# Where four DMA transpositions of the second attention step stand in SP's queue

## The chip, the cores and the metric

The kernel runs on one core of one Trainium2 chip. The metric is the device time of one execution in microseconds, as the median of several runs. The engines are TensorE (PE), VectorE (DVE), ScalarE (ACT), GpSimd (POOL) and SyncE (SP); here SP does nothing but issue DMAs, and POOL nothing but issue loads after its first few microseconds.

## What is computed

Eight sequences of 3072 rows go through an attention without softmax, gated by u, and then through a two-branch maxout layer:

```python
scores = (1/S) * z @ z.T            # S = 3072, z has 64 columns
attn   = maximum(scores, 0) ** 2
x      = u * (attn @ v)             # u and v have 256 columns
h      = maximum(x @ w1, x @ w2)    # 1024 columns
out    = h @ w_out                  # 256 columns
```

The inputs and the output are float32; the products are made in bfloat16 with float32 sums.

## The kernel before, in words

**Tiles.** A sequence is cut into 24 blocks of 128 rows, and these into 6 groups of 4 blocks. A step is one group of output rows of one sequence; there are 48, counted from n = 0, and steps 0 to 5 belong to the first sequence. Step n needs attn between its own 4 blocks and all 24 blocks of the sequence, group by group.

**Symmetry.** The scores are symmetric. Only the part on and above the diagonal is made on PE (`add_pair`, `add_diag`); ACT and DVE apply the maximum and the square, which leaves a tile `a_sb` for each step and group. A later step that needs the mirrored tile gets it by a DMA transposition, issued by SP (`do_turn`, through `sp_dma`, L83), into a tile `aT`. One transposition turns two blocks, so step n makes T(n,k) and T(n,k+2) for a group g with k = 4g, and step g reads them. For the first sequence, steps 0 to 2 make their tiles among each other directly and are added up plainly (`add_plain`). From step 3 on, the products run through a scheme with seven products in place of eight: DVE makes sums of the tiles (`add_sums`, the jobs S1 to S4 in `es`) and differences of v (`add_fold`, in `lf`), and PE makes products X (three a piece, from the tiles) and Y (four a piece, from the tiles and the sums).

**The other transpositions on SP.** Each step's u is turned (`uT`); the second weight is turned once (`w2T`), because PE multiplies it with w_out at the start (`w2o`); each later sequence's z is turned into `zT`, from which its scores are made; the diagonal group of each step is turned in place in two small pieces. SP also issues the stores of the output, 512 KB each. The loads (v, u, z and the weights) are issued by POOL (L87) and most of them wait for a given matmul (`timed`).

**Order.** The order of PE's work is written out by hand (`work`, `laid`, giving `pe_order`). All other jobs are put in order by a planner at the end of the function: each job has a cost, a lag and a due time worked out backwards from PE's plan, and the planner hands each engine the job that is ready first and, among those, the one due first. SP takes its jobs strictly in that order.

**Buffers.** A job that takes a new tile of a pool waits until all jobs of the tile that had the buffer are done, and takers of a pool follow each other in the order written in `order`. The pool of `aT` has 12 buffers (`NT`). Its order comes from a sorted list, `slots`: each turned group has a place in PE's order as its key, and so have the second weight (`w2`, `w2T`) and the two tiles of step 0's groups 4 and 5, which are kept in this pool (`a_held`) until they are turned late. Because the takers follow each other, a place in `slots` is also a place in SP's order.

The function `held` picks step 0's groups 4 and 5; their key is the place of PE 1 us into step 2, in the plan's time. All other groups have the place of the first score that makes them.

Of the kernel before, what the change touches and what calls it, by code (L numbers as in the profile page):

```python
# [11 lines left out]
def kernel(  # L12
# [29 lines left out]
    G = 4  # L42
# [215 lines left out]
    def a_key(n, g):  # L258
        return ("T", ("held", n, g)) if n < HELD and g > 3 else ("A", (n, g))
# [734 lines left out]
    for i, w in enumerate(work):  # L994
        key = w[2]
# [44 lines left out]
    def pe_job_at(ns):  # L1040
        found = [key for key, at in zip(pe_order, pe_at) if at >= ns]
        return [found[0]] if found else [pe_order[-1]]


    def at_step(b, s, us):
        return pe_job_at(starts[NG * b + s] + us * 1000)
# [160 lines left out]
    for pool in ("acc0", "acc1"):  # L1207
        order[pool].sort(key=lambda k: k[0] * 2 + k[1] if isinstance(k, tuple) else 2 * k)
    position = {key: i for i, key in enumerate(pe_order)}
    order["A"].sort(  # L1210
        key=lambda k: position.get(("score", k[0], None if k[1] == steps[k[0]].s and steps[k[0]].diag else G * k[1]), -1)
    )
    def held(key):
        return a_key(key[1], key[2] // G)[0] == "T"

    slots = sorted(
        [
            (position[at_step(0, key[1] + 2, 1)[0]] if held(key) else position.get(key, -1), k)
            for key, k in turned_order
        ]  # L1220
        + [(position.get(key, -1), ("held", key[1], k[2])) for key, k in turned_order if held(key)]
# [1 line left out]
        key=lambda x: x[0],  # L1223
# [210 lines left out]
```

## Time and profile before

| | |
|---|---|
| time, median of 3 runs | 932.8 us (932.5 to 934.61) |
| the profiled execution | 930.27 us |
| its span, first to last instruction | 928.5 us |
| PE busy | 923.0 us (99%) |
| DVE busy | 766.3 us (83%) |
| ACT busy | 682.2 us (73%) |
| POOL busy | 58.4 us (6%) |
| granted TensorE clock | 1.000 |
| mean DMA flow | 154 GB/s |
| transpositions `aT` issued by SP | 230, median 4.2 us to landing |
| transpositions `uT` | 48, median 4.6 us to landing |
| loads of v, of u | 48 each, 256 KB, median 5.3 us to landing |

The profile is one execution. Busy is the time in which an engine executes instructions; matmuls overlap each other, and their ends are modelled, so PE's waits are better read from the distances between starts. "Landing" is the moment at which a DMA's completion is told. SP's rows in the timeline give the time that SP spends on issuing a DMA; the data lands later. A window row gives, for a stretch of time, the busy time of each engine with its number of instructions, then the granted clock, the mean busy share of the 16 DMA engines and the flow in GB/s.

### The profile page before, as it was taken

How to read it: one execution, taken by the hardware profiler on the slowest of the kernel's cores; microseconds unless marked ns; L12 is line 12 of the kernel's file. 1: busy time of each engine (PE TensorE's matmuls, PEld its weight loads, DVE VectorE, ACT ScalarE, POOL GpSimd, SP SyncE). 2: the span in 40 equal slices, each digit the busy share in tenths (PEclk: the TensorE clock that was granted, in tenths of full speed). 3: DMA queues.
4: the chain of work that ended last, by engine and by line, in shares of the span. 5: the costliest groups of instructions: out<-in, count | busy, mean ns of one | idle time of the engine just before them, and what ended most of it. 6: DMA issues, size and time to landing. Idle time of an engine off the chain costs nothing.

```text
span 928.5 us, 18994 instructions
## 1 busy us (share of the span) xinstructions
PE 923.0 (99%) x7343; PEld 668.2 (72%) x7343; DVE 766.3 (83%) x1915; ACT 682.2 (73%) x825; POOL 58.4 (6%) x115
## 2 busy tenths in 40 slices
PE   9999999999999999999999999999999999999998
PEld 3367777777777777777777776777767776777786
DVE  7958997888978888888888888888898887988761
ACT  8867876778777777776877678776888658875634
POOL 2100100000000000001000010000000000000000
PEclk9999999999999999999999999999999999999999
DMA  9999999987989879998999899988898888986611
GB/s 161 151 183 180 179 186 181 158 156 136 160 172 157 151 137 180 165 152 144 151 188 153 153 146 158 172 150 153 144 166 173 149 149 149 183 154 125 121 46 68
DMA packets 372778, 142.54 MB, mean 154 GB/s; under 512 B 351184, under 2 KB 352848, under 8 KB 372688
## 3 DMA queue, kind: packets, MB, share of 16 engines
q1 hardware_dynamic: 356128, 111.60, 64.6%
q0 software_dynamic: 16560, 29.74, 22.9%
q8 instruction: 57, 0.93, 0.4%
q14 instruction: 33, 0.27, 0.1%
HBM read 59.77 MB, written 25.17 MB: 91 GB/s over the span
## 4 chain that ended last, share of the span: by engine, by line
PE 94%; DVE 3%; DMA 1%; issue 0%; ACT 0%; POOL 0%; POOLq 0%
PE s_ps L80 47%; PE acc L80 47%; DVE es L233 1%; DMA v_sb<-in_v_dram 1%; DVE a_sb L221 1%; DVE lf L236 0%; DMA o_sb<-in_z_dram 0%; DVE a_sb L233 0%; DVE xT L240 0%; DVE e L233 0%; DVE a_sb L227 0%; DVE g_sb L221 0%; DVE e L236 0%; ACT a_sb L225 0%; ACT a_sb L219 0%
## 5 line engine op out<-in xcount | busy, mean ns | idle before, releaser
L80 PEld LDWEIGHTS <-v_sb 128*128 128x128 bf16 x2304 | 223.7, 98 | 79.9 <-issue 37.7
L219 ACT ACTIVATE a_sb<-s_ps 128x1024 bf16<-128x1024 f32 (+1 forms) x231 | 211.6, 971 | 30.7 <-PE s_ps L80 28.0
L225 ACT ACTIVATE a_sb<-a_sb 128x1024 bf16<-128x1024 bf16 (+1 forms) x220 | 214.2, 1010 | 0.3
L80 PE MATMUL acc<-es,v_sb 128*128 128x256 bf16 x864 | 197.4, 274 | 0.1
L80 PE MATMUL s_ps<-w_out_sb,g_sb 128*128 128x256 bf16 x1504 | 195.0, 273 | 0.0
L219 ACT ACTIVATE g_sb<-s_ps 128x1024 bf16<-128x1024 f32 x181 | 170.9, 1029 | 13.4 <-PE s_ps L80 13.4
L233 DVE TENSOR_TENSOR es<-a_sb 128x512 bf16<-128x512 bf16 x306 | 121.1, 416 | 66.9 <-PE acc L80 66.9
L80 PEld LDWEIGHTS <-lf 128*128 128x128 bf16 x1620 | 158.3, 98 | 22.6 <-issue 0.3
L80 PE MATMUL s_ps<-xT,w_sb 128*128 128x512 bf16 x768 | 173.6, 379 | 0.0
L80 PE MATMUL acc<-es,lf 128*128 128x256 bf16 x756 | 170.8, 273 | 0.0
L80 PE MATMUL acc<-a_sb,lf 128*128 128x256 bf16 x612 | 166.9, 273 | 0.0
L80 PEld LDWEIGHTS <-g_sb 128*128 128x128 bf16 x1504 | 146.9, 98 | 17.5
L80 PE MATMUL acc<-aT,v_sb 128*128 128x256 bf16 x684 | 143.0, 273 | 0.0
L80 PE MATMUL acc<-a_sb,v_sb 128*128 128x256 bf16 (+1 forms) x740 | 138.9, 291 | 0.3 <-ACT a_sb L225 0.3
L80 PEld LDWEIGHTS <-w_sb 128*128 128x128 bf16 x768 | 75.0, 98 | 81.1 <-issue 0.3
L230 ACT COPY e<-acc 128x512 f32<-128x512 f32 x90 | 53.2, 591 | 108.9 <-PE acc L80 108.5
L221 DVE TENSOR_SCALAR a_sb<-s_ps 128x1024 bf16<-128x1024 f32 (+1 forms) x107 | 121.2, 1133 | 5.1 <-PE s_ps L80 4.8
L230 ACT COPY o_sb<-s_ps 128x512 f32<-128x512 f32 (+1 forms) x92 | 53.1, 577 | 86.3 <-PE s_ps L80 86.3
L80 PE MATMUL s_ps<-zT 64*128 64x512 bf16 (+1 forms) x684 | 92.9, 366 | 0.4 <-DVE zT L110 0.4
L227 DVE TENSOR_TENSOR a_sb<-a_sb 128x1024 bf16<-128x1024 bf16 (+1 forms) x118 | 75.0, 647 | 0.2 <-ACT a_sb L219 0.2
L80 PE MATMUL s_ps<-W2o_sb,xT 128*128 128x256 bf16 x384 | 73.4, 273 | 0.0
L80 PE MATMUL acc<-aT,lf 128*128 128x256 bf16 x252 | 68.7, 273 | 0.0
(60 smaller groups left out, 711.8 us busy)
## 6 DMA issues: line engine op xcount, KB each, us to landing
out_dram<-o_sb SPq DMA_DIRECT2D x47, 512.0 KB, 3.7
v_sb<-in_v_dram POOLq DMA_DIRECT2D x48, 256.0 KB, 5.3
u_sb<-in_u_dram POOLq DMA_DIRECT2D x48, 256.0 KB, 5.3
aT<-a_sb SPq DMA_TRANSPOSE x230, 4.2
z_sb<-in_z_dram POOLq DMA_DIRECT2D x7, 384.0 KB, 5.4
a_sb<-a_sb SPq DMA_TRANSPOSE x90, 3.2
w_sb<-in_moe_w_dram POOLq DMA_DIRECT2D x2, 512.0 KB, 9.6
uT<-u_sb SPq DMA_TRANSPOSE x48, 4.6
```

The source lines that it names most:

```text
L80: newest[0] = pin(nc.tensor.matmul(*args, **kw)).ins
L219: pin(nc.scalar.activation(out_ap, in_ap, AF.Relu))
L221: pin(nc.vector.tensor_single_scalar(out=out_ap, in_=in_ap, scalar=0.0, op=ALU.max))
L225: pin(nc.scalar.activation(ap, ap, AF.Square))
L227: pin(nc.vector.tensor_mul(ap, ap, ap))
L230: pin(nc.scalar.copy(out_ap, in_ap) if eng == "ACT" else nc.vector.tensor_copy(out_ap, in_ap))
L233: pin(nc.vector.tensor_add(*args))
```

## The change

Step 1's groups 4 and 5, which had the place of their first score as key, now get the place of PE 1.5 us into step 2. Step 0's groups 4 and 5 get the place 4 us into step 2 in place of 1 us. Everything else of the source stays.

```diff
     def held(key):
         return a_key(key[1], key[2] // G)[0] == "T"
 
+    LATE = (4, 1.5)
+
+    def late(key):
+        return key[1] < 2 and key[2] // G > 3
+
     slots = sorted(
         [
-            (position[at_step(0, key[1] + 2, 1)[0]] if held(key) else position.get(key, -1), k)
+            (position[at_step(0, 2, LATE[key[1]])[0]] if late(key) else position.get(key, -1), k)
             for key, k in turned_order
         ]
         + [(position.get(key, -1), ("held", key[1], k[2])) for key, k in turned_order if held(key)]
```

What SP issues early, in the order of both kernels ("d3" is step 3's pair of small diagonal transpositions, "w2" the second weight, "u2" the u of step 2, "s0" the store of step 0's output, "zT" two DMAs):

```
before: T(1,12) T(1,16) T(1,14) T(1,20) w2 u2 T(1,18) T(2,12) T(2,14) T(1,22) T(2,16) T(0,16) d3
        T(0,18) T(2,18) T(0,20) u3 T(0,22) u4 s0 T(2,20) T(3,16) T(3,18) d4 zT T(2,22) T(3,20)
        T(3,22) T(4,20) d5 s1 u5 T(4,22) d6 T(6,4) T(6,8) s2 u6 T(6,12) T(6,16) T(6,20)
after:  T(1,12) T(1,14) w2 u2 T(2,12) T(2,14) T(2,16) T(1,16) T(1,18) d3 T(1,20) T(1,22) T(2,20)
        T(0,16) T(0,18) T(2,18) u3 T(2,22) s0 u4 T(0,20) T(3,16) T(3,18) d4 zT T(0,22) d5 s1 u5
        T(3,20) T(3,22) T(4,20) T(4,22) d6 T(6,4) s2 T(6,8) T(6,12) u6 T(6,16) T(6,20)
```

The 12 buffers of the `aT` pool go round in the new order too: the tile of (step 0, group 5) now takes the buffer of (step 0, group 3), which step 3 reads first, in place of (step 2, group 5), and (sequence 1, step 0, group 3) no longer takes a buffer that step 5 reads.

## The prediction

> A transposition is written T(n,k) below: SP's DMA that turns blocks k and k+1 of step n; steps, groups and blocks count from 0, so the second step is n = 1.
>
> **What bounds the kernel now.** I read the page first: busy shares, then the chain that ended last.
>
> ```profile
> PE 923.0 (99%) x7343; PEld 668.2 (72%) x7343; DVE 766.3 (83%) x1915; ACT 682.2 (73%) x825; POOL 58.4 (6%) x115
> ...
> PE 94%; DVE 3%; DMA 1%; issue 0%; ACT 0%; POOL 0%; POOLq 0%
> ```
>
> TensorE is busy for 99% of the span and is 94% of the chain. A busy PE can still be waiting, because matmul ends are modelled, so the list of waits and then the start-to-start distances of the matmuls come next.
>
> ```profile
> PE zeros L80 <- DVE blank L144: 1.2, 1, 1.2
> PE s_ps L80 <- DVE zT L110: 0.4, 1, 0.4
> PE tpz L109 <- DVE z_sb L154: 0.3, 1, 0.3
> PE acc L80 <- ACT a_sb L225: 0.3, 1, 0.3
> ```
>
> All of PE's listed waits lie in the first 10 us. In the timeline of PE after that, two 256-column matmuls take 0.38 us. I looked for pairs that take longer, in the whole span:
>
> ```profile
> 130.40 0.38 PE L80 MATMUL acc<-es,v_sb 128*128 128x256 bf16 x2
> 130.62 0.27 PE L80 MATMUL acc<-a_sb,lf 128*128 128x256 bf16 x1
> 130.73 0.27 PE L80 MATMUL acc<-es,lf 128*128 128x256 bf16 x1
> 130.84 0.63 PE L80 MATMUL acc<-es,v_sb 128*128 128x256 bf16 x2
> ```
>
> The last pair lost 0.25 us. Besides it there are 0.18 us at 123.7 and 0.08 us at 68.2, and nothing else above the constant price of switching between scores and products. So stalls that could go are worth 0.51 us in this execution, and anything beyond that must come from losses which it does not show.
>
> **The time to sum against.** The profiled execution took 930.27 us (span 928.50 and 1.77 around it). The median of the runs is 932.8, 2.5 above it, and they spread over 2.1 (932.5 to 934.61). I take differences from the profile and add them to the median.
>
> **The change, part by part.** The order views of both kernels show PE, ACT and POOL unchanged; DVE has the same instructions with five of them moved by one place or a few; SP has the same DMAs in another order up to T(6,16). So no work is added or removed: everything is about when SP's transpositions land. These are SP's issues now (start, duration):
>
> ```profile
> 25.35 7.53 SPq L83 DMA_TRANSPOSE aT<-a_sb  x4
> 32.98 8.72 SPq L83 DMA_TRANSPOSE w2T_sb<-w_sb  x1
> 41.78 1.26 SPq L83 DMA_TRANSPOSE uT<-u_sb  x1
> 43.14 10.66 SPq L83 DMA_TRANSPOSE aT<-a_sb  x5
> ...
> 63.09 2.57 SPq L83 DMA_TRANSPOSE uT<-u_sb  x1
> ...
> 76.72 4.81 SPq L83 DMA_TRANSPOSE zT<-z_sb  x2
> 81.58 8.14 SPq L83 DMA_TRANSPOSE aT<-a_sb  x4
> ```
>
> *Step 1, the head of the queue.* Today T(1,12), T(1,16), T(1,14), T(1,20) go ahead of the second weight. With T(1,16) and T(1,20) gone from there, the weight's transposition moves from 33.0 to about 28.1 (its load landed at 26.7), and the third u's follows it (load landed at 31.6). Then SP meets T(2,12), whose square ends on DVE at 39.0: four finished transpositions of step 1 now stand behind that wait. Their users are far: DVE first reads T(1,16) and T(1,18) at 73.3, for step 4, and T(1,20) and T(1,22) at 92.5, for step 5; the four will land by about 58 (nine issues from 39.1 on, priced as below). Cost 0, hidden by at least 15 us.
>
> *Step 2, up to the next sequence's zT.* zT is the transposition with the least margin: its second half lands at 86.38 and PE's score row starts at 86.66, 0.28 us later. In the new order SP has 22 instructions from T(2,12) up to zT. The rows price one 8-block transposition at 1.4 us with its gap (57.83 to 59.28, 67.11 to 68.50), a pair of small diagonal ones at 2.51 and a store at 0.6: 17 x 1.4 + 2 x 2.51 + 0.6 = 29.4. Between 41.78 and 76.72 the same sum of today's 21 gives 28.0 against 34.9 measured, so loads and the store beside them cost 6.9. From 39.1 on: 39.1 + 29.4 + 6.9 = 75.4. The other bounds: T(0,20) now takes the buffer that step 3's first group frees at 68.0, so zT cannot start before 68.0 + 3 x 1.4 + 2.5 = 74.7; and if weight and u clog SP until 43.1, as long as they do today, it starts at 79.4. SP and the DMA engines have the same amount to do ahead of zT in both kernels, which speaks for 76.7. I take 75.4 to 76.7, so zT lands at 85.1 to 86.4, and PE waits as little as today: 0. The ends are 0 (PE does not wait there today, so nothing can be gained) and +2.4 (89.1 less 86.7).
>
> *Step 3, the fourth u.* DVE now stands still 2.79 us until this transposition lands at 67.7. In the new order it comes after 13 issues from 39.1 on: 11 x 1.4 + 2.51 = 17.9, and 3.9 for the two loads of that stretch (the row at 43.14 is 10.66 for five, 3.9 over their price), so it issues near 61 and lands near 65, when DVE asks for it. The DVE wait goes, but what is late next is PE itself, whose products of step 3 release DVE's next sums at 68.1. Worth at most the 0.08 us at 68.2.
>
> *Step 4, behind zT.* T(0,22) takes the place of T(2,22), which was issued at 81.58 and landed at 88.84. Its reader is nearer: DVE's sums of step 5's first group at 90.38, not those of group 2 at 96.86.
>
> ```profile
> 90.38 0.42 DVE L233 TENSOR_TENSOR es<-aT 128x512 bf16<-128x512 bf16 x1
> 90.71 0.42 DVE L233 TENSOR_TENSOR es<-a_sb,es 128x512 bf16<-128x512 bf16 x1
> ```
>
> The row after it makes the sum that PE wants at 91.81 (0.69 us to spare). So T(0,22) has 1.54 + 0.69 = 2.2 us before PE stands still: cost 0, and an end of +2.7 below. T(3,20), T(3,22) and T(4,20) move behind the store and the sixth u; T(3,22) then lands near 96.4 and is read at 98.54. T(4,22) has as many issues ahead of it as before and keeps its 1.34 us (99.19 against 100.53). T(3,20) must wait for T(0,22)'s landing, 88.8, and SP gets to it near 89.7: 0.
>
> *Step 5, step 6's transpositions.* Today T(6,12) waits for a buffer until 108.96; in the new order its buffer is free early, so it and the store ahead of it leave the stretch from 106 on, where a load of v is caught among them:
>
> ```profile
> 106.96 9.48 DMA v_sb<-in_v_dram
> ...
> 131.19 1.03 PE acc L80 x8
> ```
>
> This is the chain of waits in order of time: that load takes 9.48 us where the median load of v takes 5.3 (section 6 of the page); behind it DVE works without a gap until it makes PE late at 131. If it lands 2 us earlier, both stalls at 123.7 and 130.8 go: -0.43. If it meets as many transpositions as now: 0. I take -0.4.
>
> [...] When transpositions and a load meet, flow falls:
>
> ```profile
> 33.00:38.00 5.00, 5.00 (x29) 1.91 (x29) 5.00 (x10) 4.01 (x5) 0.00 (x0) 1.00 1.29 76
> ...
> 48.00:53.00 5.00, 5.00 (x25) 2.25 (x23) 4.46 (x10) 4.01 (x6) 0.00 (x0) 1.00 1.22 212
> ```
>
> The last two columns are the DMA share and GB/s: 76 against 212 at the same share, and T(1,14) needed 12.2 us from issue to landing in it (28.01 to 40.25). [...]
>
> **Sum:** 0 + 0 - 0.08 + 0 - 0.4 = -0.5, that is 929.8 for the profiled execution and 932.3 for the median.
>
> **Rivals.**
>
> *A, faster by more than the profile can show.* The 2.5 us between profile and median, and the spread of 2.1, are losses of executions that I do not see. If they sit at the places with no margin, which are zT (0.28), the fourth u (0.1) and the load at 107 (none), the change eases the last two and perhaps the first, and the runs fall to the profile's level: 932.8 - 2.5 = 930.3. For it: these places all lie in the stretch that the change reorders, and no later sequence shows such a stall. Against it: the gap may be a constant of unprofiled runs.
>
> *B, slower: T(0,22) late.* It is issued among the sixth u's load and zT's packets. It decides from 2.2 us of lateness on, microsecond for microsecond. With the 12.2 us of T(1,14) it lands at 81.6 + 12.2 = 93.8, 3.4 after DVE wants it, and PE loses 3.4 - 0.7 = 2.7: 935.5. Against it: T(2,22) took 7.3 in the same place.
>
> *C, slower: SP idles at the queue's head.* If the second weight holds SP until 43.1 as it does today, zT starts at 79.4, lands at 89.1, and PE waits 89.1 - 86.7 = 2.4: 935.2. For it: the load of the first weight (28.2 to 40.3) lies beside it in both orders. [...]
>
> *D, no effect.* That the order is not changed is excluded by the order views; that it changes nothing in time is part of the forecast.
>
> **How the numbers follow.** The forecast, 932.3 (its own range 931.3 to 933.6), has 0.50; A 0.28; B 0.13; C 0.09. About 0.2% (1.9 us) is what a measurement of this kernel can tell from no change, so A counts as faster (below 930.9), B and C as slower (above 934.7). For 8 in 10 the range goes from 929.9 (A's 930.3 less the 0.4 of step 5) to 935.3 (between C and B).
>
> **What would show it.** Right: zT lands before 86.7; DVE shows no wait of 2.8 us for a uT; the load at 107 lands near 112 to 114 and no pair of matmuls near 131 takes over 0.4 us. B shows as DVE waiting for aT near 90 and PE pairs stretched near 92; C as PE's first score row of step 6 late by microseconds behind zT. The prediction is wrong if PE waits for anything else between 60 and 160.

## The result, and the profile after

| | before | after |
|---|---|---|
| time, median | 932.92 us (930.67 to 934.61, 6 runs) | 942.48 us (937.11 to 943.49, 6 runs) |
| ratio after to before | | 1.0091, 95% interval 1.0073 to 1.0109 |
| the profiled execution | 930.27 us, span 928.5 | 942.54 us, span 940.8 |
| granted TensorE clock, mean | 1.000 | 0.996 |

The kernel became 0.9% slower; 932.3 was forecast, with 929.9 to 935.3 as the range for 8 in 10. The spans differ by 12.3 us. I compared the distances between matmul starts with those of before in stretches of 20 us: 0.3 of the 12.3 come up in the first 20 us, 2.8 between 60 and 80, 9.6 between 100 and 120, and behind 120 PE gains 0.4 back. So there are two places to explain, and the second is three quarters of it.

The page of the kernel after, its busy line and its chain:

```profile
PE 925.4 (98%) x7343; PEld 670.3 (71%) x7343; DVE 766.6 (81%) x1915; ACT 682.0 (72%) x825; POOL 58.4 (6%) x115
...
PE 95%; DMA 2%; SPq 1%; DVE 1%; ACT 0%; issue 0%; POOL 0%; POOLq 0%; DVEq 0%
```

The work is the same to the instruction. DMA and SP's queue, 1% and nothing in the chain of before, now hold 3%. PE's waits (what was waited for, then us in total, times, longest):

```profile
PE acc L80 <- DMA aT<-a_sb: 7.8, 1, 7.8
PE s_ps L80 <- DVE a_sb L221: 1.5, 1, 1.5
...
PE acc L80 <- DVE es L233: 0.9, 1, 0.9
```

All three are new. The first, in PE's timeline (start, duration, and in brackets the idle time with its releaser):

```profile
103.58 0.38 PE L80 MATMUL acc<-aT,v_sb 128*128 128x256 bf16 x2
111.74 0.37 PE L80 MATMUL acc<-aT,lf 128*128 128x256 bf16 x1 [7.78 <-DMA aT<-a_sb]
111.91 0.63 PE L80 MATMUL acc<-aT,v_sb 128*128 128x256 bf16 x2
112.34 0.42 PE L80 MATMUL acc<-aT,lf 128*128 128x256 bf16 x1
```

This is a product of step 5 that reads T(4,22). A matmul of 256 columns starts 0.11 us after the one before it ahead of the wait and 0.21 after it: PE comes back at half speed, to which I return at the end. What released it, in the chain in order of time, and the row of SP that issued it, the last of four:

```profile
100.90 10.80 DMA aT<-a_sb
```

```profile
91.61 1.50 SPq L83 DMA_TRANSPOSE uT<-u_sb  x1
93.20 8.96 SPq L83 DMA_TRANSPOSE aT<-a_sb  x4
```

T(4,22) took 10.8 us from issue to landing. In the kernel before it was the row

```profile
95.72 1.35 SPq L83 DMA_TRANSPOSE aT<-a_sb  x1
```

It landed at 99.19, and PE read it at 100.53: 1.34 us to spare. PE was late itself in the kernel after and wanted the tile 3.1 us after its issue, so with the 3.5 us of before it would have waited 0.4 us; the rest of the 7.8 is the longer way from issue to landing. What may have made it three times as long stands in POOL's rows of the kernel after:

```profile
100.68 0.53 POOL L87 DMA_DIRECT2D v_sb<-in_v_dram  x1 [6.88 <-PE s_ps L80]
101.20 0.54 POOL L87 DMA_DIRECT2D u_sb<-in_u_dram  x1
101.72 0.55 POOL L87 DMA_DIRECT2D v_sb<-in_v_dram  x1
```

and of the kernel before, where the same three follow PE's same matmul:

```profile
97.51 0.53 POOL L87 DMA_DIRECT2D v_sb<-in_v_dram  x1 [6.88 <-PE s_ps L80]
98.03 0.54 POOL L87 DMA_DIRECT2D u_sb<-in_u_dram  x1
98.55 0.55 POOL L87 DMA_DIRECT2D v_sb<-in_v_dram  x1
```

These three loads, called **the trio** from here on, wait for PE and so move with PE; T(4,22) moves with SP's queue. Before, T(4,22) went out 1.8 us ahead of the trio. After, the trio came 3.2 us later, T(4,22) 5.2 us later, and went out 0.2 us behind the trio's first load. The trio landed at 105.4, 110.3 and 111.6, T(4,22) at 111.7.

The second place, DVE's wait for the fourth u's transposition (u3) and SP's rows up to it:

```profile
DVE xT L240 <- DMA uT<-u_sb: 6.2, 1, 6.2
```

```profile
28.34 4.67 SPq L83 DMA_TRANSPOSE w2T_sb<-w_sb  x1
33.13 5.19 SPq L83 DMA_TRANSPOSE uT<-u_sb  x1
39.38 14.83 SPq L83 DMA_TRANSPOSE aT<-a_sb  x5
...
61.17 5.48 SPq L83 DMA_TRANSPOSE aT<-a_held  x2
66.74 1.26 SPq L83 DMA_TRANSPOSE aT<-a_sb  x1
68.09 1.28 SPq L83 DMA_TRANSPOSE uT<-u_sb  x1
```

u3 went out at 68.1, where it was 63.1 before and 61 was forecast. DVE stood still 6.2 us for it, not 2.8, and the work behind it on DVE made PE wait 1.5 us from 72.4 and 0.9 us from 74.3.

### The profile page after: what moved, and what is told of

Its sections match the earlier page's. It is cut to its first block, busy times and chain, and to the rows that moved or that the text cites. A ratio compares the mean times of both kernels' runs of the same rounds, so it can differ in the third digit from the quotient of the medians.

```text
span 940.8 us, 18990 instructions
## 1 busy us (share of the span) xinstructions
PE 925.4 (98%) x7343; PEld 670.3 (71%) x7343; DVE 766.6 (81%) x1915; ACT 682.0 (72%) x825; POOL 58.4 (6%) x115
## 4 chain that ended last, share of the span: by engine, by line
PE 95%; DMA 2%; SPq 1%; DVE 1%; ACT 0%; issue 0%; POOL 0%; POOLq 0%; DVEq 0%
PE acc L80 47%; PE s_ps L80 47%; SPq L83 1%; DMA aT<-a_sb 1%; DMA z_sb<-in_z_dram 1%; ACT g_sb L219 0%; DMA uT<-u_sb 0%; DVE es L233 0%; DVE e L233 0%; DVE xT L240 0%; DVE a_sb L221 0%; PE tpz_c L109 0%; DVE aT L233 0%; DVE a_sb L233 0%; ACT o_sb L230 0%
## 5 line engine op out<-in xcount | busy, mean ns | idle before, releaser
L233 DVE TENSOR_TENSOR es<-a_sb 128x512 bf16<-128x512 bf16 x306 | 122.0, 421 | 67.0 <-PE acc L80 66.9
L80 PEld LDWEIGHTS <-w_sb 128*128 128x128 bf16 x768 | 75.4, 98 | 81.3 <-issue 0.7
## 6 DMA issues: line engine op xcount, KB each, us to landing
w_sb<-in_moe_w_dram POOLq DMA_DIRECT2D x2, 512.0 KB, 10.2
```

What stands on the lines that cost most here:

```text
L80: newest[0] = pin(nc.tensor.matmul(*args, **kw)).ins
L233: pin(nc.vector.tensor_add(*args))
```

## The experiments

**Theory.** T(4,22) lost its place ahead of the trio. SP is late by two parts: at the queue's head (step 1's four transpositions, which now stand behind T(2,12), so that the second weight's and the third u's meet the first weight's load) and behind zT (four transpositions in a row behind the store and u5, from T(0,22)'s new place). **Rivals:** the reordering costs by itself, by late tiles or buffers, whatever the trio does; or one of the two parts carries the whole loss.

Each run compares with runs of the kernel before on the same chip: 933.14 us for e1, e2, e3 and e5; 933.19 for e4, e6, e7 and e8; 932.18 for e9 to e11; 932.86 for e12. Intervals are 95%.

### The two halves of the change, each alone

**e1_step1_only**: only step 1's groups are late; the order from zT on is that of before.

```diff
-    LATE = (4, 1.5)
+    LATE = (1, 1.5)
```

> Only step 1's groups 4 and 5 are put late; step 0's keep their place, so SP's head has the second weight and the third u in front, but T(3,20), T(3,22), T(4,20) stay ahead of the store and the sixth u as in the kernel before. Theory H (the head makes SP late, and T(4,22) then meets the three loads that PE's place releases near 100): T(4,22) is issued after 98 and lands 8 to 11 us later, PE waits 5 to 8 us near 100, time 938 to 943. Theory T (the order behind zT makes T(4,22) late): T(4,22) is issued within 2 us of PE's first product of step 5 as before, no wait over 1 us near 100, time 932 to 935, with at most the 1.7 us near 72 on top.

Measured: 935.70 us, ratio 1.0031 (1.0002 to 1.0061). u3 went out at 69.1 and PE lost 2.4 us between 60 and 80; T(4,22) went out 2.5 us ahead of the trio, because PE, and with it the trio, was later still; no wait for it. That is what theory T says.

**e2_step0_only**: only step 0's groups are late; the queue's head is that of before.

```diff
-    LATE = (4, 1.5)
+    LATE = (4,)
-        return key[1] < 2 and key[2] // G > 3
+        return key[1] < 1 and key[2] // G > 3
```

> Only step 0's groups 4 and 5 are put 3 us later; step 1's keep their place, so SP's head is that of the kernel before, and the stretch behind zT is that of the changed kernel. Theory H: the fourth u lands early enough, no wait of DVE over 3 us near 65, T(4,22) is issued near 96 and lands near 100, time 931 to 934. Theory T: T(4,22) is issued 2 us later against PE than before, meets the three loads, and PE waits 5 to 8 us near 100, time 938 to 941.

Measured: 934.33 us, ratio 1.0015 (0.9986 to 1.0043). In its profile T(4,22) went out in the same 0.1 us as the trio's first load, took 6.2 us, and PE waited 2.9, less than theory T has and more than H.

What follows: the halves cost 2.6 and 1.2 us (the second not to be told from none), 3.8 together, and the whole change 9.6. In the medians neither half carries the loss; more than the sum comes up where both meet, as a threshold such as the place ahead of the trio gives it and a sum of small delays does not. Single runs are less clear-cut: two of e1's ten took 942.2 and 944.0 us and one of e2's 941.6, at granted clocks of 0.994 to 0.996, where all six runs of the kernel after show 0.995 or 0.996. So each half alone seems to lose that place now and then (no trace of these runs is kept, and it is inferred from time and clock), and both together lose it each time. In the kept traces the halves do different things: the first costs by u3 and leaves T(4,22) its lead on the trio (2.5 us), the second takes the lead away (0.0).

### The trio alone

**e5_before_loads_sooner**: the order before the change, untouched; the trio waits for matmuls 3 to 6 us sooner.

```diff
-            add_u(n, at_step(pb, ps, 2 if pb == 0 else 4))
+            add_u(n, at_step(pb, ps, -1 if n == 6 else 2 if pb == 0 else 4))
-            v_at = [(4, 8), (4, 14), (5, 1), (5, 4), (5, 9.5), (5, 11)]
+            v_at = [(4, 8), (4, 14), (5, -2), (5, -1), (5, 9.5), (5, 11)]
```

> The kernel before, its SP order kept, with the same three loads released some 3 to 6 us sooner, so that they are under way when T(4,22) is issued near 96. Collision theory: T(4,22) takes 7 to 11 us to land in place of 3.5, PE waits 2 to 7 us near 100, time 935 to 940. If SP's lateness against PE matters and the loads do not: T(4,22) lands by 100.5, time 931.5 to 934.5.

Measured: 942.41 us, ratio 1.0098 (1.0071 to 1.0124), as slow as the change and above the 935 to 940 that the theory gave. The trio went out at 91.1, 92.8 and 95.4, T(4,22) behind it at 96.1, landing 11.6 us later; PE's waits and the place, as in the kernel after:

```profile
PE acc L80 <- DMA aT<-a_sb: 6.9, 1, 6.9
```

```profile
100.46 0.38 PE L80 MATMUL acc<-aT,v_sb 128*128 128x256 bf16 x2
107.76 0.37 PE L80 MATMUL acc<-aT,lf 128*128 128x256 bf16 x1 [6.92 <-DMA aT<-a_sb]
```

What follows: without any reordering, putting the trio ahead of T(4,22) gives the same wait for the same tile and the same loss. The rival that the order costs by itself is not needed for it.

**e7_before_loads_2us_later**: the control, the order before with the trio the other way. Two of its loads get a place 2 us later; the third keeps its place and goes out behind the first.

```diff
-            add_u(n, at_step(pb, ps, 2 if pb == 0 else 4))
+            add_u(n, at_step(pb, ps, 4 if n == 6 else 2 if pb == 0 else 4))
-            v_at = [(4, 8), (4, 14), (5, 1), (5, 4), (5, 9.5), (5, 11)]
+            v_at = [(4, 8), (4, 14), (5, 3), (5, 4), (5, 9.5), (5, 11)]
```

> The kernel before with the same shift of 2 us. If the runs of the kernel before that lie above its fastest by 2 to 7 us lose that to the same meeting, they come closer together and the median falls by 0.5 to 2 us (931 to 932.6). If not, it stays within 0.5 of 933 or rises, because v comes later.

Measured: 931.96 us, ratio 0.9993 (0.9969 to 1.0018). T(4,22) was 2.75 us ahead of the trio, took 4.5 us and had 0.9 to spare. In the profiled executions the order had enough room before and after this edit.

**e3_after_loads_later**: the kernel after, the trio 4 to 7 us later.

```diff
-            add_u(n, at_step(pb, ps, 2 if pb == 0 else 4))
+            add_u(n, at_step(pb, ps, 8 if n == 6 else 2 if pb == 0 else 4))
-            v_at = [(4, 8), (4, 14), (5, 1), (5, 4), (5, 9.5), (5, 11)]
+            v_at = [(4, 8), (4, 14), (5, 8), (5, 8), (5, 9.5), (5, 11)]
```

> The changed kernel with the three loads of v and u that are released near 100 put some 4 us later in PE's order (two of v at 8 us into step 5, u of step 6 at 8). If the collision with these loads makes T(4,22) take 10.8 us, it now lands 3 to 5 us after its issue, and PE's wait of 7.9 us shrinks to 0 to 2.5: time 933 to 937. If T(4,22) is late by SP's order alone, the wait stays over 5 us: time over 939.

Measured: 936.85 us, ratio 1.0041 (1.0023 to 1.0060). T(4,22) took 4.3 us and PE did not wait for it. Instead five loads went out between 107 and 112, the last three landed at 124 to 128, and PE lost 6 us in four waits between 123 and 135. The profiled execution is the slowest of the ten, here (941.62) and in e6 (941.58), so its losses are larger than the median's.

**e6_after_loads_2us_later**: the kernel after with e7's edit.

> The changed kernel with the three loads near 100 released only some 2 us later (the run with 4 us and more took away the wait for T(4,22), but made DVE and PE wait for v near 125 to 135). Collision theory: T(4,22) lands by 106, PE's wait there is 0 to 3 us, none over 1 us near 125 to 135, time 934 to 937. Rival: what counts is SP's lateness alone, wait over 5 us, time over 940.

Measured: 937.85 us, ratio 1.0057 (1.0037 to 1.0078). T(4,22) went out 5.7 us ahead of the trio and PE did not wait for it, but now u3's lateness cost more (DVE waited 8.0 us, and PE lost 6.9 between 60 and 80), and v landed at 124 and 126 and cost 4.2 between 120 and 140, where the expectation allowed no wait over 1 us. Part of the 5.7 us is PE's own lateness, which holds the trio back; e3 is the cleaner test.

What follows from both: with T(4,22) clear of the trio its wait goes, as the theory says, and 5 to 6 us of the 9.6 come back. The rest does not: the loads have no later place that is free, and u3 is late independent of them.

### The queue's head

**e4_after_w1_later**: the kernel after; the load of the first weight waits for a matmul about 7 us later, so that it no longer meets the second weight's transposition.

```diff
-        (lambda: w1_sb, moe_w1, "w1", (1, 3), None, "(c p) f -> p c f"),
+        (lambda: w1_sb, moe_w1, "w1", (1, 8.5), None, "(c p) f -> p c f"),
```

> The changed kernel with the first weight's load released some 7 us later in PE's order (from about 28.5 to about 36), so that it no longer lies beside the transpositions of the second weight and the third u. If the meeting of that load with the second weight's transposition is what makes SP late at the head, T(2,14) lands 2 us or more earlier, the fourth u is issued by 65 (68.1 in the changed kernel), the 1.7 us near 72 go, T(4,22) is issued 2 to 4 us earlier against PE, and the time is 932 to 937. If SP is late for its waits alone, the fourth u stays at 67 to 69 and the time at 940 to 944.

Measured: 934.48 us, ratio 1.0022 (0.9985 to 1.0058); single runs from 931.38 to 943.48. SP's rows:

```profile
29.52 3.84 SPq L83 DMA_TRANSPOSE w2T_sb<-w_sb  x1
33.47 1.24 SPq L83 DMA_TRANSPOSE uT<-u_sb  x1
39.55 11.50 SPq L83 DMA_TRANSPOSE aT<-a_sb  x5
...
66.85 1.25 SPq L83 DMA_TRANSPOSE uT<-u_sb  x1
```

The third u's transposition now takes 1.24 us in place of 5.19, and SP is free at 34.7. It then stands idle until 39.55, because T(2,12) is next and its data is not there, while four finished transpositions of step 1 wait behind it. u3 goes out at 66.9, only 1.2 us sooner. T(4,22) went out at 99.92, the trio's first at 100.00, and PE waited 2.8 us. Most of the loss is gone from the median, but not by way of u3: SP was a little earlier where a little decides. Three of the ten runs still took 941 to 943 us, at a clock of 0.996, as the kernel after does.

**e8_after_both**: the edits of e4 and e6 together.

> The changed kernel with both: the first weight's load later and the three loads 2 us later. If the two meetings are the whole loss, the time is that of the kernel before, 931 to 934; if something of the changed order costs by itself, it stays over 935.

Measured: 935.96 us, ratio 1.0025 (1.0001 to 1.0048). The time lies over 935, where something of the order costs by itself, but in the trace the meeting is still there. SP was idle from 33.6 to 39.0; T(4,22) at 99.11, the trio's first at 99.09, since PE now ran earlier too; PE waited 3.1. Moving the trio in the plan's time did not help here, because PE's own loss near 72, which delays the trio, shrank at the same time (1.3 us between 60 and 80, 6.9 in e6).

**e9_fill_gap**: step 1's four transpositions get a place right behind the second weight's and the third u's, so that SP has finished data to work on. SP's head is then w2 u2 T(1,16) T(1,20) T(2,12) T(2,14) T(1,18) T(1,22).

```diff
-    LATE = (4, 1.5)
+    LATE = ((2, 1), (1, 7.5))
-            (position[at_step(0, 2, LATE[key[1]])[0]] if late(key) else position.get(key, -1), k)
+            (position[at_step(0, *LATE[key[1]])[0]] if late(key) else position.get(key, -1), k)
```

In one point the expectation misdescribes its kernel, here and in the next two runs: `(2, 1)` is the place that step 0's groups had before the change, so from zT on the order is that of the kernel before, not after. e9 is to be read against e1.

> The order after the change with one thing altered: step 1's four transpositions T(1,16), T(1,20), T(1,18), T(1,22), which are finished by then, stand right behind the second weight's and the third u's, ahead of or among T(2,12) and T(2,14), so that they fill the time in which SP waits for T(2,12)'s data. Step 0's groups keep their late place, and the order from zT on is that of the kernel after. Theory (two losses: SP's queue stands behind T(2,12), and the second weight's meets the load of the first weight; T(4,22) then goes out with the three loads near 101): the first loss goes, the second stays; fourth u issued 63 to 66, no DVE wait above 3 us for it, T(4,22) issued 0.5 to 2 us ahead of the first of the three loads and landed in 4 to 6 us; 932.5 to 935.5. Rival (the meeting with the first weight's load alone makes SP late): fourth u issued near 68 as after the change, T(4,22) among the loads, a stall of 3 us or more near 103; 936 or more.

Measured: 935.05 us, ratio 1.0030 (1.0012 to 1.0048). The time lies in the theory's range, but the mechanism is the rival's: u3 went out at 68.6, DVE waited 6.8 us for it, and PE lost nearly 5 us between 60 and 80 by it. The second weight's and the third u's transpositions held SP for 4.99 and 6.20 us. Beside the first weight's load SP had no idle time to fill: the third u's ended at 39.71, and the next transposition started at 39.81.

**e10_fill_gap_w1_later**: e9 with e4's edit.

> As e9_fill_gap, and the load of the first weight waits for a matmul about 7 us later (as in e4_after_w1_later), so that the second weight's and the third u's transpositions are off SP before it. Theory: both losses of the queue's head are gone; SP shows no idle time above 1.5 us between 28 and 40; fourth u issued at 63 or sooner; T(4,22) 1.5 us or more ahead of the three loads, no stall of PE above 0.5 us near 72 and 103; 930.5 to 933. Rival (what stands behind zT alone makes T(4,22) late): a stall of 1 to 3 us near 102 as in e2_step0_only, 934 to 936.

Measured: 931.76 us, ratio 0.9994 (0.9972 to 1.0016). SP's rows:

```profile
28.46 4.27 SPq L83 DMA_TRANSPOSE w2T_sb<-w_sb  x1
32.84 1.24 SPq L83 DMA_TRANSPOSE uT<-u_sb  x1
34.18 15.61 SPq L83 DMA_TRANSPOSE aT<-a_sb  x6
...
61.05 2.17 SPq L83 DMA_TRANSPOSE uT<-u_sb  x1
```

The row of six hides a pause: its second transposition ends at 36.84, and T(2,12) starts at 39.51, so 2.7 us of idle time are left, more than the 1.5 expected, where e4 had 4.8. u3 at 61.1, DVE's wait for it 1.7 us, T(4,22) at 93.8 and 4.2 us ahead of the trio, and no wait of PE between 60 and 160. Moving the one load by 7 us is worth 3.3 us here (935.05 against 931.76). Taking step 1's four transpositions out of the queue's head costs nothing that can be told once the head meets no load and two of the four fill most of the gap (their place here is not the one of the change); each of the two repairs alone (e4 for the load, e9 for the gap) leaves u3 near 67 to 69.

**e11_fill_all**: e10 with e7's edit of the trio.

> As e10_fill_gap_w1_later, and the three loads of v and u near 100 wait for a matmul 2 us later. Theory: T(4,22) has 3 us or more to spare against the first of them, the loads of v land 2 us later but not as late as in e3_after_loads_later (112 or sooner for the last of the three), no stall of PE above 0.5 us between 60 and 160; 930 to 932.5, if anything beats the kernel before it is this one. Rival (the later loads are paid back by late v near 124 to 135, as in e6_after_loads_2us_later): stalls of 2 to 3 us near 130; 934 to 938.

Measured: 930.57 us (929.91 to 932.06, 10 runs), ratio 0.9982 (0.9968 to 0.9995): the first version that beats the kernel before, by 0.18%. Between 60 and 160 no distance between PE's matmul starts is more than 0.3 us over its constant price (0.11 us behind a matmul of 256 columns, 0.22 behind one of 512). The same holds for the profiled execution of the kernel before, and from 20 to 160 PE needs the same time in both within 0.1 us: the gain lies in executions of which no trace is kept.

**e12_before_both**: the order before the change, with the two shifts of loads of e11. It asks what e11's gain is due to.

> The order before the change, with both shifts of loads of e11_fill_all: the load of the first weight waits for a matmul about 7 us later, and the three loads of v and u near 98 wait for one 2 us later. It asks whether what e11_fill_all gains on the kernel before (0.18%) comes from these shifts or from the order. Theory (the shifts: what costs time is the meeting of SP's transpositions with loads, whichever order stands): the second weight's transposition no longer meets the load, the fourth u issued before 62, T(4,22) issued 4 us or more ahead of the three loads, 930 to 931.5. Rival (the order is needed as well): 931.7 to 933, as the kernel before or e7_before_loads_2us_later, with DVE still waiting 2 us or more for the fourth u.

Measured: 931.06 us (929.74 to 931.62, 12 runs), ratio 0.9981 (0.9968 to 0.9994). The same gain without any reordering. It comes from the loads; the order of step 1's transpositions is then worth nothing that can be told either way, not even through u3, for which DVE still waits 2.5 us here, as the rival had it.

### All kernels beside each other

Times from each profiled execution, in order of how far T(4,22) was ahead of the trio's first load:

| kernel | T(4,22) issued | trio's first | ahead | issue to landing | PE's wait for it |
|---|---|---|---|---|---|
| e5 | 96.10 | 91.12 | -5.0 | 11.6 | 6.9 |
| after | 100.90 | 100.68 | -0.2 | 10.8 | 7.8 |
| e8 | 99.11 | 99.09 | 0.0 | 6.0 | 3.1 |
| e2 | 98.40 | 98.39 | 0.0 | 6.2 | 2.9 |
| e4 | 99.92 | 100.00 | 0.1 | 6.2 | 2.8 |
| before | 95.72 | 97.51 | 1.8 | 3.5 | 0 |
| e1 | 99.27 | 101.78 | 2.5 | 4.7 | 0 |
| e7 | 96.51 | 99.26 | 2.8 | 4.5 | 0 |
| e11 | 95.14 | 98.40 | 3.3 | 4.9 | 0 |
| e9 | 98.75 | 102.61 | 3.9 | 6.2 | 0 |
| e12 | 93.77 | 97.80 | 4.0 | 5.9 | 0 |
| e10 | 93.77 | 97.98 | 4.2 | 6.6 | 0 |
| e6 | 99.31 | 105.02 | 5.7 | 6.8 | 0 |
| e3 | 99.17 | 107.01 | 7.8 | 4.3 | 0 |

PE waits in the five with 0.1 us or less, and in none of the nine with 1.8 or more. The durations follow the loads that are in flight. In e6, e9, e10 and e12 the load of v before the trio had not yet landed when T(4,22) went out (in e10 it ran from 90.57 to 95.71), and it took 5.9 to 6.8 us; in before, e1 and e7 that load had landed, in e3 and e11 it landed within 0.3 us, and it took 3.5 to 4.9. Beside the trio's first load it took 6.0 to 6.2, and behind it 10.8 and 11.6.

## Why the prediction was wrong, step by step

*Step 4 failed, and it is the one that cost most.* It says that T(4,22) "has as many issues ahead of it as before and keeps its 1.34 us". The count was right. But SP needed 16.5 us from zT's end to T(4,22) in place of 14.2, and started 3 us late from the head. The 2.3 us do not come from T(0,22), which held SP for 3.8 where T(2,22) had held it for 3.6. They come from T(3,22), 3.7 in place of 1.7, and T(4,20), 2.3 in place of 1.3, which now stand beside a load of v (93.3 to 98.6), while the sixth u's took 1.5 in place of 2.6. e2, e4 and e8, which share this order behind zT, show 16.2 to 16.4 as well; e1, e7 and e9 to e12, with the order of before there, 13.3 to 14.6. (Where loads fall otherwise it differs: 14.3 in e3 and 12.9 in e6 with this order, 16.1 in e5 with that of before.) PE, and with it the trio, was 3.2 us late by then, as much as the head had cost, so it is these 2 us that took the lead on the trio. And the margin that mattered was not the 1.34 us to PE but the 1.8 us to the trio, which I had not looked for: what a transposition costs behind loads I weighed for T(0,22) alone. The sum has 0 for this step; between the profiled executions it cost 9.6 us, 7.9 of wait and 1.6 of lower clock behind it.

*Step 3 failed, by its sizes.* u3 goes out "near 61": 17.9 us of issues and 3.9 for loads, from 39.1 on. T(2,12) did go out at 39.4, but 28.7 us passed up to u3, so what I had put down to loads took 10.8, not 3.9 (3.7 by the price of 1.4 us). SP did not wait in between; its issues were longer. I carried over a term from a stretch that meets loads less. The sum has -0.08 for this step; the stretch from 60 to 80 cost 2.8. The landings show what happened: the first weight's load landed at 43.1 (40.3 before), w_out at 50.8 (47.8) and the u load at 52.2 (49.1), each 3 us later.

*Step 1* holds for its tiles: nobody waited for T(1,16) to T(1,22). Its "Cost 0" leaves out SP itself. The second weight's transposition at 28 meets the load that starts at 28.5, which it had met before too, and now the third u's meets it as well (5.2 us on SP in place of 1.3); the time that SP stands there is not saved by moving whom it stands for. e4 and e10 show the remainder: without the load, a gap of 5 us at T(2,12), and u3 at 61 only when most of that is filled.

*Step 2.* zT started at 80.0, not 75.4 to 76.7, beyond the upper bound of 79.4. PE still did not wait for it (it landed at 89.51, and the score row started at 89.82), because PE was itself 3 us late. So "0" came out for another reason than mine.

*Step 5* has the right number, by luck as far as the runs show: the two slow pairs near 124 and 131 have no counterpart in the kernel after, a gain of 0.4 us that the large loss hides, and the load of v that follows took 5.0 us in place of 9.5. But this load went out at 119.7, not 107, because PE had stood still, and so met other transpositions; and e5, e10 and e12, which have SP's order of before in this place, gain the same 0.4 (e11, with that order too, does not). That the buffer of T(6,12) did it is not shown.

*The rivals.* B did not happen: T(0,22) took 7.5 us and landed at 92.0, while DVE read it in its order at 93.5. C has the right culprit, the first weight's load at the queue's head, with the wrong course: SP was past the second weight and the third u at 38.3, not 43.1, and lost its time behind T(2,12). zT kept its place against PE; u3 paid, and T(4,22) in part.

A's guess that the distance between the profile and the median is made of losses at narrow margins fits e11 and e12: they do nothing but widen margins, and their medians, 930.6 and 931.1, lie near where A put the profile's level (930.3). They do not make the best executions better: the lowest runs are 929.9 and 929.7, against 929.6 and 929.8 of the kernel before on the same chips; the highest fall from 935.8 to 932.1 and 931.6. Of the 102 runs of the kernel before that stand beside e1 to e12, 24 show a granted clock of 0.998 or less, and each of these took 933.7 us or more; all 22 runs of e11 and e12 show 0.999 or 1.000. In the kept traces the clock is lower only at or behind waits of PE (0.50 from 108.3 to 115.1 in the kernel after, nowhere in the span of the one before) and at the very end, so the gap is not a constant: some executions of the kernel before lose at a wait that its profiled execution does not have. Which wait, no trace shows.

The size that B works with came up for another tile: T(4,22) took 10.8 us among three loads, near the 12.2 that I had kept for T(0,22).

*The method.* I checked each moved transposition against its reader. A chain of late DMAs can also slip behind transfers that another engine releases, as T(4,22) did, from 1.8 us ahead of the trio to 0.2 behind its first load; the list of what to check is readers and neighbours.

**What stays open.** How much time the second half (T(0,22) behind zT) costs cannot be told: e2's interval takes in no change, and the whole change with both repairs of the head and a free trio was not run. Nor do the runs show where in the DMA engines T(4,22) waits. The packets of the trace show two stages: for 2.1 us (102.3 to 104.4) nothing of SP's queue moves while the loads' packets do; then both move, the loads at 40 to 56 packets of 2 KB each us, where they had 67 to 95 in the kernel before with hardly anything of SP's queue beside them. T(4,22) landed at 111.7, 0.1 us after the trio's last load; whether it waited for these loads to end or shared bandwidth with them, no run here separates.

## What to carry to other kernels

When a DMA is moved in a queue, look for its margin not only to its reader but to each transfer that another engine's progress releases nearby: here SP's queue and PE's order drifted past each other by 2 us, and 3.5 us to landing became 10.8. The meeting of transpositions with the first weight's load was not removed by changing which transposition meets it (the third u's then took 5.2 us on SP in place of 1.3), and getting past it early helped little while the next entry of the queue had no data (in e4 SP stood from 34.7 to 39.55 at T(2,12), and u3 gained 1.2 us). Where several margins are narrow, shift the loads first: 0.2% came from two such shifts (e12), nothing that could be told from the order.

## What I had not expected of the hardware

PE's long wait cost more than its length, 9.6 us for a wait of 7.8. The kernel after, windows (us, then the busy time of PE, PEld, DVE, ACT and POOL, then the granted clock, the DMA share and GB/s):

```profile
104.00:107.00 3.00, 0.00 (x0) 0.00 (x0) 2.63 (x7) 1.59 (x2) 0.00 (x0) 1.00 1.30 187
107.00:108.00 1.00, 0.00 (x0) 0.00 (x0) 0.00 (x0) 0.00 (x0) 0.00 (x0) 1.00 1.03 115
108.00:109.00 1.00, 0.00 (x0) 0.00 (x0) 0.00 (x0) 0.00 (x0) 0.00 (x0) 0.65 1.40 165
109.00:110.00 1.00, 0.00 (x0) 0.00 (x0) 0.00 (x0) 0.00 (x0) 0.00 (x0) 0.50 1.39 107
...
112.00:115.00 3.00, 3.00 (x14) 1.78 (x13) 0.31 (x1) 0.58 (x1) 0.00 (x0) 0.50 1.17 342
115.00:116.00 1.00, 1.00 (x6) 0.44 (x5) 1.00 (x5) 0.35 (x1) 0.00 (x0) 0.93 1.23 261
```

The clock falls to 0.50 during the wait, at 108.3 by the share of that window, and comes back at 115.1, 3.4 us after PE went on: about 1.6 of the 9.6 us. The half clock lasted 6.8 us. In e5, where PE waited 6.9 us, it lasted 10.2 (102.9 to 113.1), and in e2 3.4:

```profile
104.00:105.00 1.00, 0.41 (x4) 0.37 (x4) 0.12 (x1) 0.00 (x0) 0.00 (x0) 1.00 1.13 211
105.00:106.00 1.00, 1.00 (x9) 0.80 (x8) 0.00 (x0) 0.00 (x0) 0.00 (x0) 0.71 1.09 184
...
108.00:109.00 1.00, 1.00 (x5) 0.32 (x3) 0.67 (x4) 0.92 (x1) 0.00 (x0) 0.58 1.09 451
109.00:110.00 1.00, 1.00 (x6) 0.47 (x5) 0.00 (x0) 0.70 (x2) 0.00 (x0) 1.00 1.15 261
```

There it fell at 105.4, when PE, after a wait of 2.9 us, was working again, and came back at 108.8: 3.4 us of matmuls at half speed, by my estimate some 1.7 us lost, behind a wait of under 3 us. It need not come: e4's wait of 2.8 us left the clock at 1.00 (1.000 over the whole execution), while in e9, where no wait was longer than 2.2 us, it was half from 75.4 to 78.8 (0.998 over the whole execution). So the length of a wait alone did not tell whether the clock falls; what does, these runs do not show.
